# Two layers of attention over a key-value cache on one core: the last pair's sums moved ahead of the held chunks, a place of its own for five rows of wo, PV at the end of a turn, a K tile in four pieces

## The chip, the core and the metric

The kernel runs on one core of a Trainium2 chip. The core has a matrix engine (PE in the profile, with its weight loads as PEld), a vector engine (DVE), a scalar engine (ACT), a general engine (POOL), a queue that issues transfers (SP), and sixteen DMA engines that move data between the chip's memory and the core's own memory (SBUF). Matrix products land in a third, small memory (PSUM). The engines run side by side, each in the order of its own instructions, and wait for each other by semaphores. The metric is the device time of one execution in microseconds (us); less is better.

## What is computed

One token for each of two sequences goes through two layers. A layer adds an attention over a cache of 16384 keys in 32 heads, and then a block of two small matrices with a shift and an MLP with 4608 columns. Cut to what matters here:

```python
B, Sq, D = 2, 1, 576
H, Sk, Dh = 32, 16384, 128          # k_cache, v_cache: (B, H, Sk, Dh) in bf16

def _A_ref(x, k_cache, v_cache, wq, wo):
    q = (x @ wq).reshape(B, Sq, H, Dh).transpose(0, 2, 1, 3)
    scores = jnp.einsum("bhqd,bhkd->bhqk", q, k_cache) * (Dh ** -0.5)
    p = _softmax(scores, axis=-1)
    o = jnp.einsum("bhqk,bhkd->bhqd", p, v_cache)
    return o.transpose(0, 2, 1, 3).reshape(B, Sq, H * Dh) @ wo

def _B_ref(x, w1, w2, w3, w4):      # h = gelu(layernorm(x) @ w1), shifted by a token
    x1 = x + hs                     # hs = shifted h @ w2; with one token the shift leaves zeros
    return x1 + _gelu(_layernorm(x1) @ w3) @ w4

x = x + _A_ref(_layernorm(x), K, V, wq, wo)
x = x + _B_ref(_layernorm(x), w1, w2, w3, w4)
x = x + _A_ref(_layernorm(x), K, V, wq, wo)      # the same cache and weights again
x = x + _B_ref(_layernorm(x), w1, w2, w3, w4)
```

Both layers read the whole of K and V: 2 x 2 x 268 MB, which is nearly all of the 1093 MB that the profile counts.

## The kernel before, in words

**Tiles.** The 64 pairs of sequence and head are taken two heads at a time: 32 *pairs* in a layer. The K tile of a pair fills the 128 partitions, 64 for each head, with 256 keys of 128 numbers each in a partition: 65536 bytes in a partition, 8.39 MB in all. The V tile is as large. A tile is counted in 256 *blocks* (a block is one key in each partition, 256 bytes), and these in 8 groups of 32. SBUF holds three tile places (slots). K tiles take slots 0 and 1 in turn, V tiles have slot 2 alone, so the V tile of a pair can only be loaded when the V tile before it has been read.

**A pair's work** is written in `pair`. The blocks of the odd groups are scored on PE: `transposed` turns a chunk of 8 blocks (L1356), ACT copies it from PSUM to a small buffer (`evacuate`, L1362), and `scores` multiplies it with q (L1379), two chunks behind (`LEAD = 2`). There are 16 such chunks. The blocks of the even groups are scored on DVE: `dots` multiplies 16 blocks with q (L1391) and sums each over its 128 numbers (L1395), eight times in a pair; these are the *sums* of the title. Then come the maximum (`first_max` L1400, `softmax_max` L1408 and L1412, with a reduction over the partitions on POOL, L1414), the exponentials on ACT (L1423, L1429), and the q of the next pair (`q_column` L1305, `q_spread` L1312, `q_copy` L1317, which writes `qb`, read by the next pair's multiplications). The weights p then meet V one turn later: `pv` (L1448) is 256 small matmuls, and it stands in the turn of the pair after, behind the first three chunks:

```python
            if c == self.LEAD and s > 0:
                self.landed("v", self.order(l)[s - 1], False)
                for g in range(8):
                    self.pv(l, s - 1, g)
                self.tick()
```

So turn s holds the scores of pair s and the PV of pair s-1. `keep_o` (L1436) on DVE takes the result of PV away. Pairs 1 to 30 of layer 0, and 1 to 31 of layer 1, are turns of a real loop on PE, ACT and DVE (`Graph.loop`); `HEAD` gives the place of the loop's first PE instruction in a block of 256 instructions. SP and POOL have no loop; their instructions are written out. POOL passes on the landing of a tile (`landed`) to PE and DVE.

**Loads.** `plan_all` lists all loads in one order, and each carries the place that it fills. `Store.pump` adds the next load of the list to SP's queue as soon as, in the order of the program, the place is free (`used` and `release` free it in steps of two blocks). SP issues in that order and waits ahead of each load until the last readers of the place are done; a load that waits holds back all loads behind it. Where the last reader signals only its own engine or another one, SP waits for the next instruction of that engine that has a signal for all (`_stand_in`): for a multiplication of `dots` that is `first_max`. In a layer the order is K of pair s, V of pair s-1, K of pair s+1, and so on, and after the last V the weights wo, (w1,) w3, w4, and in layer 0 the wq of layer 1.

**The end of layer 0** is `closing` (pair 31, out of the loop) and `last_head` (PV of pair 31 and the product with wo). Pair 31's K and V stay in SBUF for layer 1, which starts with them, and so does the larger part of pair 30's K. To have more work early in layer 1, `ahead(l, HOLD)` turns the first four chunks of pair 31's K (blocks 0 to 31) a second time and leaves them in PSUM: the *held chunks*. That gives their cells free for a piece of wo. The place list of layer 0's wo has 76800 for the third piece (4608 bytes long); slot 1, where pair 31's K lies, starts at 73216, so the piece covers blocks 14 to 31. In `closing` the order is: sixteen chunks with half of PV 30 behind the eighth, then the held chunks, then the second half of PV 30, and then the eight `dots`. As the first two `dots` read blocks 0 to 31 and stand behind the load in the program, they wait for it, and read in blocks 14 to 31 what it wrote.

**The end of layer 1** is the last turn of the loop and `last_head`. wo comes in five pieces to slot 2: three of 8 rows, one of five rows and one of three (`WO_CUT = 5`; a row is 1152 bytes). The piece of five rows starts 3 rows ahead of the end of the 32 rows, so that it reaches two rows into the place of w1, which is next in the list:

```python
        self.plan_heads(1, [a, a + r8, a + 2 * r8, a + 4 * r8 - row * (self.HG - self.WO_CUT), a + 3 * r8])
        a += 4 * r8
        self.plan_small("w1", 1, self.w1, a, (0, 64))
```

w3's first two parts follow in slot 2, and the rest of w3 and all of w4 go to slot 0.

**The start of layer 1** is `opening` (pair 31 once more, from what was held), and then turn 1 with pair 30. The first tiles of the layer come in pieces (`FIRST`): what is missing of pair 30's K, then K of the third pair in eight pieces, V of pair 30 in three, and K of the fourth pair in two.

Of the kernel before, what the change touches and what calls it, by code (L numbers as in the profile page):

```python
# [356 lines left out]
class KB:  # L357
# [29 lines left out]
        [(0, 32768), (32768, 32768)],  # L387
# [166 lines left out]
    def plan_all(self):  # L554
# [38 lines left out]
        self.plan_heads(1, [a, a + r8, a + 2 * r8, a + 4 * r8 - row * (self.HG - self.WO_CUT), a + 3 * r8])  # L593
# [509 lines left out]
    def attention(self, l):  # L1103
        n = self.NP
        if l == 0:
            self.store.claim("kt", 0, self.AUX)
            self.q_column(0)
            self.q_spread(self.q_col, "q_col")
            self.q_copy()
            self.landed("k", self.order(l)[0], True)  # L1110
            self.pair(l, 0)
        else:
            self.opening(l)
        first = self.g.mark()
        end = n if l else n - 1
        for s in range(1, end):
            if l == 0 or s > 1:
                self.landed("k", self.order(l)[s], True)
            self.pair(l, s)
        self.g.loop(first, end - 1, 2, self.HEAD[l], self.TILE // 2 if l else -self.TILE // 2)  # L1120
# [14 lines left out]
    def pair(self, l, s):  # L1135
# [3 lines left out]
        def scores(c):  # L1139
            self.scores(self.kt[c % self.NKT], self.kt_keys(c % self.NKT), self.chunk_at(c), self.q_col, "q_col", ("s", c),  # L1140
                        last=c == 15)
        for c in range(16):
# [5 lines left out]
            if c == self.LEAD and s > 0:  # L1148
                self.landed("v", self.order(l)[s - 1], False)
                for g in range(8):  # L1150
                    self.pv(l, s - 1, g)
                self.tick()
        for c in range(16 - self.LEAD, 16):
            scores(c)
        for i in range(8):
# [10 lines left out]
    def closing(self, l):  # L1166
# [5 lines left out]
        self.landed("k", u, True)  # L1172

# [3 lines left out]
        for c in range(16):  # L1177
# [8 lines left out]
            if c == 7:  # L1186
                self.landed("v", v, False, (0,))
                for g in range(4):
                    self.pv(l, s - 1, g)
        for c in range(16 - self.LEAD, 16):  # L1190
            scores(c)
        self.ahead(l, self.HOLD)
        self.landed("v", v, False, (half,))
        for g in range(4, 8):
            self.pv(l, s - 1, g)
        self.tick()
        for i in range(8):
            self.dots(l, u, 2 * (i // 2) * self.GROUP + i % 2 * self.DB, i * self.DB)
        self.first_max(self.NB // 2)
# [334 lines left out]
```

## Time and profile before

| | |
|---|---|
| median of three runs | 2602.24 us (2601.66 to 2602.53) |
| the profiled execution | 2603.98 us, its span 2602.3 us |
| PE busy | 1623.4 us (62%) |
| DVE busy | 1901.5 us (73%) |
| ACT busy | 1173.3 us (45%) |
| DMA | 1093.05 MB, 420 GB/s over the span |
| mean granted PE clock | 0.642 |

The span runs from the first to the last instruction; the execution's own time is 1.7 us longer. Times within the trace count from the span's start. A busy share is a mean over stages that have different limits; in a stage the wait that ends last is what counts. A row of the timeline has the start, the duration, the engine, the line and the operation, and in brackets the idle time before it and what ended that. In a row of the windows the engines' busy times stand in the order PE, PEld, DVE, ACT, POOL, and the last three numbers are the granted PE clock, the share of the DMA engines and the GB/s that they moved.

### The profile page before, as it was taken

The page shows a single profiled execution, that of the slowest core. Times are in us where ns is not written, and L with a number is a line of the kernel's source. Part 1 is how long each engine was busy: PE and PEld are TensorE (multiplying, and loading weights), DVE is VectorE, ACT ScalarE, POOL GpSimd, SP SyncE. Part 2 cuts the span into 40 slices and gives each one's busy share as a digit, 9 for nine tenths or more (in the row PEclk, how much of TensorE's full clock was granted, in tenths as well). Part 3 has the DMA queues.
Part 4 walks back from the last instruction along what each step waited for, and adds up shares of the span by engine and source line. Part 5 has one row for each costly group of instructions (what it writes and reads, how often), then busy time and mean ns, then how long its engine had stood idle before and what let it go on. Part 6 is the DMA issues. An engine that isn't in the chain of part 4 may idle for free.

```text
span 2602.3 us, 82753 instructions
## 1 busy us (share of the span) xinstructions
PE 1623.4 (62%) x34418; PEld 1476.8 (57%) x34418; DVE 1901.5 (73%) x1598; ACT 1173.3 (45%) x1757; POOL 29.7 (1%) x101
## 2 busy tenths in 40 slices
PE   3657656656656656657268657657656656656656
PEld 2656556655655655656257546556556655655656
DVE  4887877877777777785428887877877877777772
ACT  2445445435435435435135445345445435435433
POOL 0000000000000000000000000000000000000000
PEclk9566666667666666656556667566666666656665
DMA  9999999999999999999489999999999999999997
GB/s 416 431 434 434 434 433 435 428 433 434 435 433 435 433 434 434 432 430 428 185 327 419 435 435 431 425 433 435 435 435 435 434 435 433 429 428 435 435 435 296
DMA packets 29364, 1093.05 MB, mean 420 GB/s; under 512 B 3210, under 2 KB 4876, under 8 KB 9612
## 3 DMA queue, kind: packets, MB, share of 16 engines
q1 hardware_dynamic: 29324, 1092.45, 97.5%
q8 instruction: 33, 0.54, 0.1%
q14 instruction: 7, 0.06, 0.0%
HBM read 1092.44 MB, written 0.00 MB: 420 GB/s over the span
## 4 chain that ended last, share of the span: by engine, by line
DMA 76%; PE 18%; issue 4%; ACT 1%; SPq 0%; DVE 0%; POOLq 0%; POOL 0%; DVEq 0%
DMA mem<-in_A_v_cache_dram 73%; PE mps L1448 17%; DMA mem<-in_B_w_dram 3%; SPq L99 0%; ACT mem L1362 0%; DMA mem<-in_A_wq_dram 0%; DMA mem<-in_A_k_cache_dram 0%; PE tps L1356 0%; DMA mem<-in_A_wo_dram 0%; PE sps L1001 0%; PE sps L928 0%; PE sps L1282 0%; PE mps L1001 0%; PE sps L1026 0%; ACT p L1429 0%
## 5 line engine op out<-in xcount | busy, mean ns | idle before, releaser
L1362 ACT ACTIVATE mem<-tps 128x1024 bf16<-128x1024 bf16 x996 | 981.8, 1027 | 1085.9 <-PE tps L1356 1071.6
L1395 DVE TENSOR_REDUCE s_dve<-prod 128x16 f32<-128x2048 bf16 x504 | 1152.2, 2286 | 17.3
L1356 PE MATMUL tps<-ident,mem 128*128 128x128 bf16 x8096 | 987.4, 259 | 55.8 <-issue 54.6
L1448 PE MATMUL mps<-p,mem 128*128 128x2 bf16 x16384 | 449.7, 165 | 639.3 <-POOLq L205 629.1
L1391 DVE TENSOR_TENSOR prod<-mem,qb 128x2048 bf16<-128x2048 bf16 x506 | 619.8, 1225 | 298.0 <-ACT qb L1317 189.2
L1356 PEld LDWEIGHTS tps<-ident,mem 128*128 (+1 forms) x8096 | 735.2, 110 | 177.7 <-issue 65.9
L1448 PEld LDWEIGHTS mps<-p,mem 128*128 128x128 bf16 x16384 | 444.3, 103 | 644.6 <-POOLq L205 634.0
L1379 PE MATMUL sps<-q_col,mem 128*128 128x2 bf16 x8064 | 367.2, 168 | 47.0 <-ACT mem L1362 44.6
L1379 PEld LDWEIGHTS sps<-q_col,mem 128*128 128x128 bf16 x8064 | 341.7, 102 | 55.5 <-ACT mem L1362 51.8
L1408 DVE TENSOR_REDUCE mx<-sps 64x1 f32<-64x128 f32 x128 | 37.1, 290 | 249.6 <-PE sps L1379 247.6
L1423 ACT ACTIVATE mx<-mx 64x1 f32<-64x1 f32 x128 | 25.7, 201 | 211.8 <-POOL mx L1414 210.3
L1312 PE MATMUL sps<-ident,q_col 128*128 128x128 bf16 x64 | 17.9, 279 | 119.3 <-DVE q_col L1305 119.3
L1312 PEld LDWEIGHTS sps<-ident,q_col 128*128 128x128 bf16 x64 | 6.6, 103 | 125.0 <-DVE q_col L1305 125.0
L1414 POOL PARTITION_ALL_REDUCE mx<-mx x64 | 25.0, 391 | 2512.7 <-DVE mx L1412 2512.7
L1429 ACT ACTIVATE p<-s_dve,mx 64x128 bf16<-64x128 f32 x126 | 50.3, 399 | 2.4
L1429 ACT ACTIVATE p<-sps,mx 64x128 bf16<-64x128 f32 (+1 forms) x130 | 46.1, 354 | 0.8
L928 PE MATMUL sps<-xn,mem 128*128 128x2 bf16 x544 | 21.3, 173 | 18.1 <-DMA mem<-in_B_w_dram 9.5
L1048 PE MATMUL sps<-share,prod 128*128 128x48 bf16 (+1 forms) x32 | 1.7, 195 | 48.1 <-DVE share L663 48.1
L928 PEld LDWEIGHTS sps<-xn,mem 128*128 128x128 bf16 x544 | 20.0, 119 | 19.2 <-DMA mem<-in_B_w_dram 10.1
L1048 PEld LDWEIGHTS sps<-share,prod 128*128 128x128 bf16 x32 | 1.3, 110 | 48.6 <-DVE share L663 48.6
L1317 ACT ACTIVATE qb<-sps 128x128 bf16<-128x128 f32 x65 | 18.0, 277 | 23.3 <-PE sps L1312 22.2
L670 ACT ACTIVATE sc<-sc 128x2 f32<-128x2 f32 x8 | 1.6, 203 | 57.5 <-DVE sc L667 57.5
(112 smaller groups left out, 304.4 us busy)
## 6 DMA issues: line engine op xcount, KB each, us to landing
mem<-in_A_v_cache_dram SPq DMA_DIRECT2D x5, 4096.0 KB, 18.8
mem<-in_A_k_cache_dram SPq DMA_DIRECT2D x10, 1024.0 KB, 7.9
mem<-in_A_wq_dram SPq DMA_DIRECT2D x8, 1024.0 KB, 16.4
mem<-in_A_k_cache_dram SPq DMA_DIRECT2D x2, 4096.0 KB, 16.7
mem<-in_B_w_dram SPq DMA_DIRECT2D x14, 576.0 KB, 7.3
mem<-in_B_w_dram SPq DMA_DIRECT2D x7, 864.0 KB, 17.9
mem<-in_B_w_dram SPq DMA_DIRECT2D x4, 1152.0 KB, 9.8
mem<-in_A_wo_dram SPq DMA_DIRECT2D x6, 576.0 KB, 15.4
```

Source lines behind the costliest of these rows:

```text
L928: ins = pe.matmul(out[:, m * B:(m + 1) * B], lhsT=buf[:, c:c + 127 * d + 1:d], rhs=self.xn[:, k, :], start=first and m == lo, stop=False, ...
L1312: self.pe(lambda pe: pe.matmul(self.sps[1][:, 256:384], lhsT=q[:, :], rhs=self.ident[:, :], start=True, stop=True, skip_group_check=True), ...
L1356: ins = pe.transpose(out[:, j * 128:(j + 1) * 128], self.g.slide(pe, self.mem, at + j * 128, 128), self.ident[:, :])
L1362: self.act(lambda e: e.activation(out=self.kt[k], in_=self.tps[t][:, :].rearrange("p (i c) -> p i c", i=self.CH), func=ACT.Copy), reads=[( ...
L1379: ins = pe.matmul(out[:, c0 + j, :], lhsT=kt[:, j, :], rhs=q[:, 0:128:64], start=True, stop=True, skip_group_check=True)
L1391: self.dv(lambda e: e.tensor_tensor(out=prod, in0=self.g.slide(e, self.mem, at, DB * 128).rearrange("p (j d) -> p j d", d=128), in1=qbc, o ...
L1395: self.dv(lambda e: e.tensor_reduce(out=sd[:, c0:c0 + DB], in_=prod, axis=AX.X, op=ALU.add), reads=["prod"], writes=[sk], to="vector")
L1408: self.dv(lambda e, p=p, a=a: e.tensor_reduce(out=self.mx[p, 1:2], in_=self.sps[0][p, a:a + n], axis=AX.X, op=ALU.max), reads=[("sps", 0)] ...
L1414: self.pool(lambda e: e.partition_all_reduce(self.mx[:, 4:6], self.mx[:, 2:4], channels=128, reduce_op=ROP.max), reads=[("mx2", 0), ("mx2" ...
L1423: self.act(lambda e, p=p, h=h: e.activation(out=self.mx[p, 6:7], in_=self.mx[p, 4 + h:5 + h], func=ACT.Copy, scale=-self.scale), reads=["m ...
L1429: self.act(lambda e, p=p, h=h, src=src, lo=lo, k=k, l=l: e.activation(out=self.p[p, h, lo:lo + k], in_=src, func=ACT.Exp, bias=self.mx[p, ...
L1448: ins = pe.matmul(self.mps[:, 448:450], lhsT=buf[:, j * 128:(j + 1) * 128], rhs=self.p[:, :, col], start=g == 0 and j == 0, stop=g == 7 an ...
```

## The change

There are four edits.

1. In `closing` the eight `dots` and `first_max` stand right behind the landing of pair 31's K, ahead of the chunks. The two halves of PV 30 stand behind the eighth and the twelfth chunk, each followed by a `tick` (one small matmul that carries a signal), so both precede the held chunks.
2. In layer 1 wo's piece of five rows starts where the third piece ends, and the piece of three rows behind it. Together they fill the 32 rows, and nothing reaches into w1's place.
3. In `pair`, PV of the pair before stands behind all chunks and their scores. Turn 1 of layer 1 alone keeps it behind the third chunk; it is taken out of the loop for that, so layer 1's loop has 30 turns, from pair 2 on, and its first slot changes (`flip`).
4. In `FIRST`, the fourth K tile of layer 1 comes in four pieces of 16384 bytes in a partition, where it came in two of 32768.

```diff
     FIRST = [
         REST,
         [(8192 * i, 8192) for i in (0, 1, 3, 5, 7, 2, 6, 4)],
         [(0, 8192), (8192, 24576), (32768, 32768)],
-        [(0, 32768), (32768, 32768)],
+        [(16384 * i, 16384) for i in range(4)],
     ]
...
-        self.plan_heads(1, [a, a + r8, a + 2 * r8, a + 4 * r8 - row * (self.HG - self.WO_CUT), a + 3 * r8])
+        self.plan_heads(1, [a, a + r8, a + 2 * r8, a + 3 * r8, a + 3 * r8 + row * self.WO_CUT])
...
         else:
             self.opening(l)
+            self.pair(l, 1, self.LEAD)
         first = self.g.mark()
-        end = n if l else n - 1
-        for s in range(1, end):
-            if l == 0 or s > 1:
-                self.landed("k", self.order(l)[s], True)
+        for s in range(l + 1, l + n - 1):
+            self.landed("k", self.order(l)[s], True)
             self.pair(l, s)
-        self.g.loop(first, end - 1, 2, self.HEAD[l], self.TILE // 2 if l else -self.TILE // 2)
+        self.g.loop(first, n - 2, 2, self.HEAD[l], -self.TILE // 2)
...
-    def pair(self, l, s):
+    def pair(self, l, s, at=None):
...
+        def ahead():
+            self.landed("v", self.order(l)[s - 1], False)
+            for g in range(8):
+                self.pv(l, s - 1, g)
+            self.tick()
         for c in range(16):
...
-            if c == self.LEAD and s > 0:
-                self.landed("v", self.order(l)[s - 1], False)
-                for g in range(8):
-                    self.pv(l, s - 1, g)
-                self.tick()
+            if c == at:
+                ahead()
         for c in range(16 - self.LEAD, 16):
             scores(c)
+        if s > 0 and at is None:
+            ahead()
...
     def closing(self, l):
...
         self.landed("k", u, True)
+        for i in range(8):
+            self.dots(l, u, 2 * (i // 2) * self.GROUP + i % 2 * self.DB, i * self.DB)
+        self.first_max(self.NB // 2)
...
-            if c == 7:
-                self.landed("v", v, False, (0,))
-                for g in range(4):
+            if c in (7, 11):
+                h = (c - 7) // 4
+                self.landed("v", v, False, (h * half,))
+                for g in range(4 * h, 4 * h + 4):
                     self.pv(l, s - 1, g)
+                self.tick()
         for c in range(16 - self.LEAD, 16):
             scores(c)
         self.ahead(l, self.HOLD)
-        self.landed("v", v, False, (half,))
-        for g in range(4, 8):
-            self.pv(l, s - 1, g)
-        self.tick()
-        for i in range(8):
-            self.dots(l, u, 2 * (i // 2) * self.GROUP + i % 2 * self.DB, i * self.DB)
-        self.first_max(self.NB // 2)
         self.keep_o(s - 1)
```

## The prediction

> **What bounds the kernel now.** I read the page's slices first, then windows around each slice that is below the rest, then the timelines of the engines in these windows and the waits of SP's queue.
>
> ```profile
> GB/s 416 431 434 434 434 433 435 428 433 434 435 433 435 433 434 434 432 430 428 185 327 419 435 435 431 425 433 435 435 435 435 434 435 433 429 428 435 435 435 296
> ...
> 1044.50:1083.20 38.70, 24.34 (x519) 22.51 (x517) 29.64 (x24) 18.00 (x27) 0.38 (x1) 0.63 1.00 434
> 1245.00:1255.00 10.00, 8.86 (x181) 8.59 (x181) 0.00 (x0) 0.00 (x0) 0.00 (x0) 0.67 0.41 151
> 1273.00:1311.00 38.00, 8.17 (x270) 8.04 (x271) 27.84 (x26) 5.80 (x15) 1.23 (x1) 0.50 0.00 1
> 2556.70:2570.00 13.30, 10.44 (x331) 10.07 (x328) 2.53 (x16) 0.00 (x0) 0.00 (x0) 0.50 0.09 25
> 2570.00:2597.00 27.00, 13.74 (x340) 12.99 (x340) 4.31 (x31) 5.56 (x11) 2.32 (x13) 0.50 1.01 405
> ```
>
> In the loops the DMA engines are full: a turn of 38.7 us moves its two tiles at 434 GB/s with a share of 1.00, while no engine is busy for more than 30 of the 38.7. So a turn can't get shorter, and time lies only where the DMA stands still: 38 us between the layers (1 GB/s), some 6 us just ahead of that (151 GB/s), and 12.5 us near the end (13.3 us at 25 GB/s hold 0.8 us of transfer). A tile takes half a turn, 19.35 us.
>
> Why the 38 us: DVE.
>
> ```profile
> 1198.91 7.01 PE L1448 MATMUL mps<-p,mem 128*128 128x2 bf16 x256 [11.38 <-POOLq L205]
> 1221.29 0.23 DVE L1305 COPY q_col<-q_f 128x128 bf16 x1
> 1235.10 0.83 PE L1448 MATMUL mps<-p,mem 128*128 128x2 bf16 x26 [1.36 <-issue]
> 1252.11 0.33 SPq L99 DMA_DIRECT2D mem<-in_A_v_cache_dram  x1
> 1268.44 1.22 DVE L1391 TENSOR_TENSOR prod<-mem,qb 128x2048 bf16<-128x2048 bf16 x1 [46.92 <-DMA mem<-in_A_wo_dram]
> 1294.75 2.29 DVE L1395 TENSOR_REDUCE s_dve<-prod 128x16 f32<-128x2048 bf16 x1
> 1298.08 0.32 DVE L1412 TENSOR_TENSOR mx<-mx 64x1 f32<-64x1 f32 x2
> 1304.36 6.83 PE mps L1448 x256
> 1311.19 1.16 PE sps L1001 x40
> ```
>
> DVE ends its loop at 1221.5 and then waits 46.9 us, for a landing of wo. By the code that is the piece over blocks 14 to 31, which the program loads ahead of the sums. The sums run from 1268.4 to 1297.0 (28.6 us), and maximum, exponentials, PV 31 (1304.4) and the product with wo (1311.2) follow in a chain. All further loads hang on that product, so the DMA is idle.
>
> **Edit 1, the sums first (T1).** They now need only pair 31's K and `qb`. V29 had landed when PV 29 began (1198.91, freed by POOL), so K31 lands 19.35 us later, at 1218.3, V30's halves at 1227.9 and 1237.6. `qb` isn't later than K31, since the turn ends earlier (edit 3, below). The sums end at 1218.3 + 28.6 = 1247. PE: chunks come each 1.07 us (below), so half a PV (3.5) can start at 1227.9 and the other at 1237.6, each with the 1.36 of idle "issue" that this row shows, which is instruction supply; the remaining chunks, scores and held chunks end at 1248 to 1252. V31's second half, issued at 1252.1 before, is issued at about 1242.5, inside the transfer of the first, which closes the hole at 1245 to 1255; it lands at 1237.6 + 19.35 = 1256.9. Maximum at 1249.4 in place of 1298.4, PV 31 six us later, at 1255.4, its second half at 1258.9; end 1262.4, with a stall of 1.4 1263.8. Against 1311.2 that is **T1 = -47.4**. What is late next is V31's landing: had the sums ended at 1253, the end would be the same within a microsecond or two. The cost that moves: wo's piece over blocks 14 to 31 must now wait for `first_max` (1247) and PE's instruction behind the held chunks (1253), with three pieces behind it in SP's queue. That is covered by V31, in flight until 1256.9, and the two pieces ahead; six pieces (3.5 MB, 8 us) land by 1265, as the product reaches them. Without that cover it would cost up to 8. Bounds: -48.8 without a stall; -40 with two stalls of 2.1 and 3.5 (rows below) and 3 of waiting for wo.
>
> **Edit 2, wo's five rows (T4).**
>
> ```profile
> SPq L99 <- PE sps L1001: 35.3, 1, 35.3
> ...
> 2529.39 3.36 SPq L99 DMA_DIRECT2D mem<-in_A_wo_dram  x5
> 2567.69 13.63 SPq L99 DMA_DIRECT2D mem<-in_B_w_dram  x15
> ...
> 2527.46 7.02 PE L1448 MATMUL mps<-p,mem 128*128 128x2 bf16 x256 [11.25 <-POOLq L205]
> 2553.87 4.02 PE L1448 MATMUL mps<-p,mem 128*128 128x2 bf16 x144
> 2559.26 3.13 PE L1448 MATMUL mps<-p,mem 128*128 128x2 bf16 x112 [1.38 <-issue]
> 2571.34 0.17 DVE L660 TENSOR_TENSOR xn<-prod,sc 128x10 bf16<-128x10 f32 x1 [0.27 <-ACT sc L670]
> 2575.77 1.73 PE L928 MATMUL sps<-xn,mem 128*128 128x2 bf16 x36 [4.02 <-DMA mem<-in_B_w_dram]
> 2578.62 1.72 PE L928 MATMUL sps<-xn,mem 128*128 128x2 bf16 x36 [1.13 <-DMA mem<-in_B_w_dram]
> ```
>
> SP waited 35.3 us for a product with wo (L1001), with fifteen weight loads behind it; the DMA idled 12.5 us. Without the overlap w1 and w3's first parts go out behind wo at PV's end (2534), the rest at the last `first_max` (by 2544), all ahead of wo's end at 2556.7. So **T4 = -12.5**. The transfer (27 us at 405 GB/s) still bounds: PV 31 starts at V31's landing (2527.5 + 19.35 = 2546.8) and ends at 2555, `xn` follows in 9 us as now (2562.4 to 2571.3), at 2564, when w3's second piece lands; a piece costs PE 1.7 us and the DMA 2.85 (the two rows of L928 start so far apart), so PE catches up. Bounds: -13.3, and -9 if it doesn't quite.
>
> **Edit 3, PV last.** The rows that carry it are those of the first turns, of layer 0 and then of layer 1.
>
> ```profile
> 72.17 3.39 PE L1356 MATMUL tps<-ident,mem 128*128 128x128 bf16 x24 [0.62 <-issue]
> 81.39 3.57 PE L1448 MATMUL mps<-p,mem 128*128 128x2 bf16 x128 [2.13 <-issue]
> 88.42 0.61 PE L1448 MATMUL mps<-p,mem 128*128 128x2 bf16 x17 [3.46 <-issue]
> 88.92 1.01 PE L1356 MATMUL tps<-ident,mem 128*128 128x128 bf16 x8
> 89.98 1.01 PE L1356 MATMUL tps<-ident,mem 128*128 128x128 bf16 x8
> 89.09 0.33 SPq L99 DMA_DIRECT2D mem<-in_A_v_cache_dram  x1
> 105.37 0.38 PE L1379 MATMUL sps<-q_col,mem 128*128 128x2 bf16 x8 [0.71 <-ACT mem L1362]
> 105.78 0.61 DVE L1408 TENSOR_REDUCE mx<-sps 64x1 f32<-64x128 f32 x2 [1.48 <-PE sps L1379]
> 110.17 1.22 DVE L1391 TENSOR_TENSOR prod<-mem,qb 128x2048 bf16<-128x2048 bf16 x1 [3.17 <-ACT qb L1317]
> 115.16 7.01 PE L1448 MATMUL mps<-p,mem 128*128 128x2 bf16 x256 [3.28 <-POOLq L205]
> ...
> 1402.10 1.16 SPq L99 DMA_DIRECT2D mem<-in_A_k_cache_dram  x2
> 1405.04 3.33 PE L1356 MATMUL tps<-ident,mem 128*128 128x128 bf16 x24 [0.86 <-POOLq L205]
> 1415.48 0.33 SPq L99 DMA_DIRECT2D mem<-in_A_v_cache_dram  x1
> 1416.35 12.97 ACT L1362 ACTIVATE mem<-tps 128x1024 bf16<-128x1024 bf16 x13 [6.92 <-PE tps L1356]
> 1443.30 7.01 PE L1448 MATMUL mps<-p,mem 128*128 128x2 bf16 x256 [0.71 <-POOLq L205]
> ```
>
> In the steady turn PV last costs nothing. K lands at T; DVE's eight sums take 29.6 (DVE's time in the window of 38.7), and from the maximum to the next pair's first multiplication go 4.4 (105.78 to 110.17), so the next turn is ready at T + 34 of 38.7: a margin of 4.5. PE: sixteen chunks at 1.07 (88.92 to 89.98) and the last scores to T + 18.6, V lands at T + 19.35, PV ends at T + 26.4, when the next V load is issued, as now; the DMA wants it at T + 38.7, a margin of 12. I take **T7 = 0**. In the first turns it costs something, because there the turn runs late and PV holds the V load.
>
> Layer 0, turn 1 (T2): V1 is issued at 89.1, waits behind K2, and has landed at 115.1, so its transfer started at 95.7. With PV last, the other thirteen chunks start at 76.0 (three chunks, 3.4, and a score from 72.2 on) where they started at 88.9; they took 16.9 us (to 105.75), so PV begins at 92.9. It takes 7.0 in the loop, and in this first pass 2.1 and 3.5 more, idle at "issue". The queue is empty this time from 95.7 on, for which the nearest row is the 1.38 near the end (DMA idle); I take 8.4. PV ends at 101.3, V1 is issued 0.2 later, and data flow 1.5 after an issue (at the end: issue at 2567.7, and 0.8 us of transfer by 2570). The DMA stands from 95.7 to 103.0: **T2 = +7.3**, between 3.5 (thirteen chunks in 14.5, as ACT's 12.97 for thirteen copies with the scores behind gives, and no stall) and 11.5 (both stalls). It is paid once: turn 2 starts by DVE, as now, and its PV ends at 133 (first chunk 107, as now, + 18.6 + 7.0), ahead of K3's end at 141.
>
> Layer 1, turn 2 (T3): the V load issued at 1415.5 has landed by 1443.3, so it started at 1423.9. With PV last the thirteen chunks start at 1408.6, end at 1423.1 to 1425.5, PV ends 7.0 to 8.4 later, in the loop's first pass; with issue and start 1.7: 1434.3. **T3 = +10.4**, between 7.9 and 15.8.
>
> By the Trainium skill (Runtime: NRT & Kernel Launch, "Instruction fetch mechanics") crossing a 16 KiB boundary of code is mostly hidden; the first pass above does not bear it out. By that rule T1 would be -48.8, T2 5.9, T3 9, and the sum would give 2556.
>
> **Edit 4, four pieces (T6).** Both pieces are issued together at 1402.1, behind `first_max`, for which SP waits whatever the piece; four will be too, at 0.58 us each, with the first under way. **T6 = 0**, between -1.5 (the gap at that place closes) and +1.2.
>
> **Sum.** -47.4 - 12.5 + 7.3 + 10.4 = -42.2, on a span of 2602.3. The profiled execution took 2603.98, the median is 2602.24, so the durations stand for the median within 0.1%. Forecast: 2560.0 us. The bounds add up to -52 and -20.5: 2550 to 2582. From run to run the times differ by under 0.05%, so 0.2% (5 us) is what I call a change.
>
> **Rivals.**
> - *The starts cost nothing*: V1 and its counterpart hide behind something I don't see; 2602.2 - 59.9 = 2542. Against it: SP's queue holds no load that could pass them. 0.08.
> - *The gains are partly given back*: instruction supply stalls PE in `closing`, `last_head` and both first passes, and the bounds all fall badly; 2582. The stalls of 2.1 and 3.5 speak for it. 0.16.
> - *Slower: the sums still start late.* If another landing or signal ahead of the sums takes the place of wo's, T1 is zero and 2602.2 + 17.7 - 12.5 = 2607. It decides as soon as T1 is under 5 us. Against it: by the code the first multiplication needs K31 and `qb` alone. 0.06.
> - *Slower: the turn no longer fits.* DVE's chain of 34 us would have to grow by over 4.5; each microsecond beyond costs 60 turns, so 0.7 beyond eats the whole gain, and one gives 2620. Against it: no instruction is added to the chain, and PV's end (T + 26.4) is ahead of `keep_o`'s turn (T + 30). 0.05.
>
> **Chances.** The forecast has 0.65, its own range being 2552 to 2569; with the second rival it fills 2550 to 2582. I give 2546 to 2582. Faster by over 0.2%: 0.65 + 0.08 + 0.16 = 0.88, rounded; slower 0.10; the same 0.02.
>
> **What would show it.** In the changed trace DVE's wait for wo should be gone, and the sums of pair 31 should start within 2 us of its K's landing; the window without transfer between the layers should shrink from 38 us to under 4; the 25 GB/s window near the end should vanish, with the weight loads issued ahead of V31's landing; and two new windows without transfer, 5 to 11 us long, should stand near 96 us and in layer 1's third pair, each ended by PV's end. Turns of 38.7 us throughout would bear out T7. Wrong it would be if turns are longer, or if DVE still waits in `closing`.

## The result, and the profile after

| | before | after |
|---|---|---|
| median | 2601.95 us (2599.72 to 2602.53) | 2560.77 us (2560.33 to 2562.96) |
| ratio | | 0.9845, interval 0.9828 to 0.9862 |
| span of the profiled execution | 2602.3 us | 2558.6 us |
| DVE busy | 1901.5 us | 1896.2 us |
| DMA | 1093.05 MB, 420 GB/s | 1093.13 MB, 427 GB/s |
| mean granted PE clock | 0.642 | 0.678 |

The forecast was 2560.0 us. The changed kernel moves the same data and does the same work; the span of its profiled execution is 43.7 us shorter, because the DMA stands still for less time. The medians differ by 41.2 us: the profiled execution of the kernel before took 2603.98 us, 2 us over its median. These are the slices of the page and some windows around its weak places (columns as in the prediction):

```profile
GB/s 413 379 429 440 426 443 426 441 428 435 433 430 439 426 442 427 441 428 433 401 408 378 426 442 427 434 434 427 442 426 442 427 441 428 434 434 428 441 426 383
...
90.00:95.00 5.00, 3.23 (x116) 3.05 (x113) 4.79 (x4) 1.02 (x1) 0.00 (x0) 0.64 0.65 279
95.00:100.00 5.00, 3.94 (x142) 3.87 (x143) 4.82 (x3) 0.00 (x0) 0.00 (x0) 0.50 0.02 3
100.00:105.00 5.00, 0.80 (x31) 0.71 (x27) 4.68 (x8) 0.00 (x0) 0.00 (x0) 0.50 0.82 292
1386.00:1389.00 3.00, 3.00 (x116) 3.00 (x114) 2.82 (x3) 0.00 (x0) 0.00 (x0) 0.50 0.02 5
1440.00:2490.00 1050.00, 672.72 (x13974) 591.37 (x13972) 805.12 (x626) 511.80 (x736) 10.22 (x27) 0.68 1.00 433
```

The slices of 185 and 327 GB/s in the middle are 401 and 408 now, and the last one went from 296 to 383. Two slices that were nearly full (431 and 419), the second (379) and the twenty-second (378), have a hole each, at 95 to 100 us and around 1387 us. In between the steady turns keep the DMA full (a share of 1.00, 433 GB/s over 1050 us).

The timeline of the changed kernel where the 38 us without transfer stood (DVE, PE, then SP's queue):

```profile
1226.36 1.23 DVE L1393 TENSOR_TENSOR prod<-mem,qb 128x2048 bf16<-128x2048 bf16 x1 [7.36 <-POOLq L205]
1252.68 2.29 DVE L1397 TENSOR_REDUCE s_dve<-prod 128x16 f32<-128x2048 bf16 x1
1256.66 0.32 DVE L1414 TENSOR_TENSOR mx<-mx 64x1 f32<-64x1 f32 x2
...
1246.10 3.58 PE L1450 MATMUL mps<-p,mem 128*128 128x2 bf16 x128 [2.30 <-POOLq L205]
1262.53 4.27 PE L1450 MATMUL mps<-p,mem 128*128 128x2 bf16 x152
1268.61 2.91 PE L1450 MATMUL mps<-p,mem 128*128 128x2 bf16 x104 [1.81 <-issue]
1274.52 0.59 PE L1001 MATMUL sps<-share,mem 128*128 128x2 bf16 x16 [2.36 <-issue]
...
1239.54 10.54 SPq L99 DMA_DIRECT2D mem<-in_A_v_cache_dram  x2
1250.11 25.35 SPq L99 DMA_DIRECT2D mem<-in_A_wo_dram  x8
1362.22 2.22 SPq L99 DMA_DIRECT2D mem<-in_A_k_cache_dram  x4
```

DVE no longer waits 46.9 us for wo. It waits 7.4 us for POOL's word that pair 31's K has landed, and sums from 1226.4 to 1255.0. The maximum stands at 1256.7, PV 31 starts at 1262.5 and ends at 1271.5. The fourth K tile of layer 1 is issued at 1362.2 instead of 1402.1.

### The profile page after: what moved, and what is told of

It is laid out like the page before. It is cut to its first block, busy times and chain, and to the rows that moved or that the text cites. A ratio compares the mean times of both kernels' runs of the same rounds, so it can differ in the third digit from the quotient of the medians.

```text
span 2558.6 us, 82601 instructions
## 1 busy us (share of the span) xinstructions
PE 1630.7 (64%) x34419; PEld 1441.1 (56%) x34419; DVE 1896.2 (74%) x1598; ACT 1206.9 (47%) x1757; POOL 30.8 (1%) x101
## 2 busy tenths in 40 slices
DMA packets 29658, 1093.13 MB, mean 427 GB/s; under 512 B 3242, under 2 KB 4908, under 8 KB 9644
## 4 chain that ended last, share of the span: by engine, by line
DMA 64%; DVE 18%; PE 11%; issue 5%; ACT 1%; DVEq 0%; POOL 0%; POOLq 0%; SPq 0%; ACTq 0%
DMA mem<-in_A_v_cache_dram 38%; DMA mem<-in_A_k_cache_dram 25%; DVE s_dve L1397 12%; PE mps L1450 9%; DVE prod L1393 6%; PE tps L1358 1%; DMA mem<-in_B_w_dram 1%; PE sps L928 0%; PE sps L1001 0%; DMA mem<-in_A_wq_dram 0%; PE mps L1001 0%; DVEq L131 0%; ACT p L1431 0%; DVE mx L1402 0%; DVEq L126 0%
## 5 line engine op out<-in xcount | busy, mean ns | idle before, releaser
L1358 PE MATMUL tps<-ident,mem 128*128 128x128 bf16 x8096 | 999.4, 246 | 400.1 <-POOLq L205 395.4
L1364 ACT ACTIVATE mem<-tps 128x1024 bf16<-128x1024 bf16 x996 | 1009.4, 1025 | 345.7 <-PE tps L1358 331.0
L1381 PE MATMUL sps<-q_col,mem 128*128 128x2 bf16 x8064 | 358.1, 167 | 48.1 <-ACT mem L1364 45.9
L1381 PEld LDWEIGHTS sps<-q_col,mem 128*128 128x128 bf16 x8064 | 322.8, 99 | 57.4 <-ACT mem L1364 56.4
L1410 DVE TENSOR_REDUCE mx<-sps 64x1 f32<-64x128 f32 x128 | 36.5, 285 | 6.7 <-PE sps L1381 4.7
L928 PE MATMUL sps<-xn,mem 128*128 128x2 bf16 x544 | 20.9, 173 | 11.4 <-DMA mem<-in_A_wq_dram 8.6
L1438 DVE COPY o_acc<-mps 128x2 f32 (+1 forms) x64 | 10.2, 160 | 22.8 <-PE mps L1450 20.8
L1431 ACT ACTIVATION_READ_ACCUMULATOR p<-sps,mx (+1 forms) x130 | 24.4, 188 | 0.0
```

What stands on the lines that cost most here:

```text
L928: ins = pe.matmul(out[:, m * B:(m + 1) * B], lhsT=buf[:, c:c + 127 * d + 1:d], rhs=self.xn[:, k, :], start=first and m == lo, stop=False, ...
L1358: ins = pe.transpose(out[:, j * 128:(j + 1) * 128], self.g.slide(pe, self.mem, at + j * 128, 128), self.ident[:, :])
L1364: self.act(lambda e: e.activation(out=self.kt[k], in_=self.tps[t][:, :].rearrange("p (i c) -> p i c", i=self.CH), func=ACT.Copy), reads=[( ...
L1381: ins = pe.matmul(out[:, c0 + j, :], lhsT=kt[:, j, :], rhs=q[:, 0:128:64], start=True, stop=True, skip_group_check=True)
L1410: self.dv(lambda e, p=p, a=a: e.tensor_reduce(out=self.mx[p, 1:2], in_=self.sps[0][p, a:a + n], axis=AX.X, op=ALU.max), reads=[("sps", 0)] ...
L1431: self.act(lambda e, p=p, h=h, src=src, lo=lo, k=k, l=l: e.activation(out=self.p[p, h, lo:lo + k], in_=src, func=ACT.Exp, bias=self.mx[p, ...
```

## The experiments

The first four make one edit, or a part of one, on the kernel before; the others alter the changed kernel. Runs 2, 3 and 4 keep the order in which pair 31's first two sums read wo's bytes; in all the others they read K, as in the changed kernel.

**1. Only the sums first.**

```diff
         self.landed("k", u, True)
+        for i in range(8):
+            self.dots(l, u, 2 * (i // 2) * self.GROUP + i % 2 * self.DB, i * self.DB)
+        self.first_max(self.NB // 2)
...
-        for i in range(8):
-            self.dots(l, u, 2 * (i // 2) * self.GROUP + i % 2 * self.DB, i * self.DB)
-        self.first_max(self.NB // 2)
```

> The kernel before with one thing changed: in closing, the eight dots and first_max stand right behind the landing of pair 31's K. PV keeps its places. Theory 1 (the wait for wo's piece is what held the sums, and nothing takes its place): DVE's 46.9 us of waiting go, the sums run from about 1224 to 1253; V31's second half is still issued at 1252, because the second half of PV 30 stands behind the held chunks, so it lands near 1264 and PV 31 ends near 1269 instead of 1311: 2602 - 42 = 2560 us (2556 to 2564), and a hole of some 6 us in the transfers ahead of it stays. Theory 2 (the gain comes from PV standing last, which lets a pair's work end ahead of the next landing; without it another wait takes the place of this one): 2590 or more.

Measured: 2563.59 us, ratio 0.9856 (0.9839 to 0.9872). Just inside the range. The first sum and the next tile's issue, in the timeline of this kernel:

```profile
1224.29 1.23 DVE L1391 TENSOR_TENSOR prod<-mem,qb 128x2048 bf16<-128x2048 bf16 x1 [2.82 <-ACT qb L1317]
...
1361.30 1.27 SPq L99 DMA_DIRECT2D mem<-in_A_k_cache_dram  x2
```

The issue moved from 1402.1 to 1361.3, by 40.8 us (by 38.6 against run 4, below). Here the sums don't wait for the tile but for `qb`, since PV, early in the turn before, pushed that turn's end back. The median is 37.2 us below the kernel before beside it, where the whole change gains 41.2: nearly the whole gain lies in this half of edit 1.

**2. Only wo's place.** One line: the place list of the five pieces, as in the diff above.

> The kernel before with only the place of wo's five rows in layer 1 changed. Theory 1 (the overlap with w1's place is the only reason for the 12.5 us without transfer near the end): the weight loads go out ahead of V31's landing, the hole goes, and as PV 31 starts as late as before (2553.9) the vector xn is ready at 2571 or, with instruction supply slower beside a full queue, at 2575; from there to the end the changed kernel takes 18.4: 2590 to 2594 us. Theory 2 (the hole is only moved, because PE and not the transfer sets the end once the loads are early): 2597 or more.

Measured: 2594.99 us, ratio 0.9979 (0.9970 to 0.9989), 5.8 us against the 2600.79 of the kernel before beside it. That is a gain, 1 us short of the range and under half of the 12.5 us that the prediction gave to this edit. The hole itself is gone: the DMA moves 403 and 421 GB/s in the two stretches of 10 us from 2550 on. But PV 31 starts no earlier than before (2551.79 us), and from `xn` on PE waits for no piece of the weights, so PE sets the end, as theory 2 has it. Where the rest lies is shown by run 5.

**3. Only PV last**, with layer 1's first turn out of the loop.

> The kernel before with only PV moved to the end of the turn (turn 1 of layer 1 out of the loop with its early PV, as in the changed kernel); closing, wo's place and the pieces are as before. Theory 1 (PV last costs the two holes in the first turns, 7.8 and 8.8 us, and gives back the lag at the ends of the layers: closing starts 4 to 5 us earlier in the transfers' time, and PV 31 of layer 1 some 7 us): +16.6 - 4.9 - 6.7 = +5, that is 2607 us (2602 to 2612), with the holes near 95 us and in layer 1's third pair. Theory 2 (PV last is what gains): under 2590.

Measured: 2610.84 us, ratio 1.0040 (1.0025 to 1.0054): the edit alone makes the kernel slower, by some 10 us, at the upper end of the range. Against the trace of run 4, which is the kernel before in all but its four pieces, it loses 7.7 us in layer 0's first turn and 8.1 in layer 1's third pair, and wins back 4.6 between the layers and only 2.8 in the tail.

**4. Only the four pieces.**

> The kernel before with only the fourth K tile of layer 1 in four pieces. Theory 1 (all pieces wait for the same first_max): all four are issued within 2.3 us at 1402, the hole of 1.5 us there stays, 2602 us within 2. Theory 2 (smaller pieces start earlier): the hole goes and 1.5 to 3 us with it.

Measured: 2601.26 us, ratio 1.0001 (0.9991 to 1.0010). No effect, as forecast. The issue of the four pieces, and PV 31 of layer 1, in the timeline of this kernel:

```profile
1399.86 1.84 SPq L99 DMA_DIRECT2D mem<-in_A_k_cache_dram  x4
...
2553.87 6.98 PE L1448 MATMUL mps<-p,mem 128*128 128x2 bf16 x256
```

Up to this issue runs 2 and 4 do what the kernel before does, and both issue at 1399.9 us. So the 1402.1 of the kernel before holds some 2.2 us that belong to its one profiled execution and not to the kernel.

**5. All but PV last**: the changed kernel with PV early in every turn.

```diff
-            self.pair(l, s)
+            self.pair(l, s, self.LEAD)
         self.g.loop(first, n - 2, 2, self.HEAD[l], -self.TILE // 2)
```

> The changed kernel with PV behind the third chunk in every turn, as before the change; the loops, the sums first, wo's place and the four pieces stay as changed. Theory 1: the holes of 7.8 and 8.8 us in the first turns go, and the lag at the layers' ends comes back (closing starts 4 us later in the transfers' time, which V31's landing partly covers; PV 31 of layer 1 7 us later, which the full queue partly covers): 2561 - 16.6 + 1 to 8 = 2545 to 2553 us, faster than the changed kernel. Theory 2 (the gain needs PV last): 2561 or more.

Measured: 2555.19 us, ratio 0.9823 (0.9807 to 0.9839): 5.6 us faster than the changed kernel (5.2 by the two spans), though 2 us short of the range. The two intervals overlap, but all four times lie below all four of the changed kernel (2554.0 to 2555.8 against 2560.3 to 2563.0). Without edit 3 the change is better. The timeline of this kernel (SP's queue, then PE at the end):

```profile
1202.51 41.48 SPq L99 DMA_DIRECT2D mem<-in_A_v_cache_dram  x4
1358.18 3.25 SPq L99 DMA_DIRECT2D mem<-in_A_k_cache_dram  x4
2486.89 3.36 SPq L99 DMA_DIRECT2D mem<-in_A_wo_dram  x5
...
2485.00 6.98 PE L1450 MATMUL mps<-p,mem 128*128 128x2 bf16 x256 [11.43 <-POOLq L205]
2511.14 3.99 PE L1450 MATMUL mps<-p,mem 128*128 128x2 bf16 x144
```

Against it, and by the same issues, the changed kernel is late by 8.0 us at the end of layer 0 (1210.46), by 4.0 at 1362.22, by 11.4 at 2498.27 and by 5.2 at the end of the span. So edit 3 costs 8.0 and 7.3 us in the two holes, and gives 3.9 back between the layers and 6.2 in the tail (2.8 in run 3, where edit 2 is missing). The tail: with PV early, PE stands 11.4 us before V of pair 30 has landed, with thirteen chunks of the last pair behind that wait, and PV 31 starts only at 2511.1.

**6. PV early in the first turns only**: two more turns of each layer written out with PV early, the loops (28 turns) with PV last.

```diff
+        for s in range(l + 1, l + 3):
+            self.landed("k", self.order(l)[s], True)
+            self.pair(l, s, self.LEAD)
         first = self.g.mark()
-        for s in range(l + 1, l + n - 1):
+        for s in range(l + 3, l + n - 1):
```

> The changed kernel with PV early (behind the third chunk) in turns 1 and 2 of layer 0 and 1 to 3 of layer 1, written out ahead of the loops; from there on PV last, in loops of 28 turns. Theory 1 (the holes come from the V load that waits for a late PV, and a turn wins 4 us on the transfers until it has caught up): both holes go, nothing comes back, 2561 - 16.6 = 2544 us (2541 to 2548). Theory 2 (the holes belong to the first pass through a loop's code, not to PV's place): they stay, one pass later, 2556 or more.

Measured: 2556.03 us, ratio 0.9825 (0.9809 to 0.9841). A miss: the rival's range. The holes at 95 and 1387 us are gone, but others stand in the first turns of the loops. Windows and timeline of layer 1:

```profile
1455.00:1459.00 4.00, 1.75 (x66) 1.66 (x63) 3.82 (x3) 0.00 (x0) 0.00 (x0) 0.50 0.40 168
1459.00:1463.00 4.00, 2.72 (x96) 2.64 (x96) 1.44 (x2) 0.00 (x0) 0.00 (x0) 0.50 0.02 4
...
1430.81 3.24 PE L1361 MATMUL tps<-ident,mem 128*128 128x128 bf16 x24 [3.21 <-issue]
1453.18 3.57 PE L1453 MATMUL mps<-p,mem 128*128 128x2 bf16 x128 [0.43 <-issue]
1460.19 2.70 PE L1453 MATMUL mps<-p,mem 128*128 128x2 bf16 x95 [3.44 <-issue]
1523.73 6.99 PE L1453 MATMUL mps<-p,mem 128*128 128x2 bf16 x256 [0.89 <-POOLq L205]
```

In the loop's first pass PE is idle at "issue" inside PV; two passes later (the last row) the same 256 matmuls run without a break. Two causes were open: these stalls, or the lag with which the turn begins.

**7. The second half of PV 30 behind the held chunks again**, as in the kernel before, with all else changed.

> The changed kernel with the second half of PV 30 in closing back behind the held chunks; the sums stay first. Theory 1 (V31's second half is then issued about 12 us later and its landing sets PV 31's end): a hole of 5 to 7 us in the transfers near 1258, 2561 + 6 = 2567 us (2563 to 2571). Theory 2 (the sums and the softmax set PV 31's start, V31's landing has room): 2561.

Measured: 2562.78 us, ratio 0.9854 (0.9838 to 0.9871): 2 us behind the changed kernel, which is less than a measurement tells apart, and by the time nearer to the rival. The trace shows theory 1's mechanism at a smaller size (SP's queue, PE, and a window):

```profile
1255.21 0.33 SPq L99 DMA_DIRECT2D mem<-in_A_v_cache_dram  x1
...
1268.89 3.58 PE L1452 MATMUL mps<-p,mem 128*128 128x2 bf16 x128 [3.02 <-POOLq L205]
...
1250.00:1260.00 10.00, 7.29 (x176) 6.83 (x173) 8.95 (x15) 2.06 (x10) 1.23 (x1) 0.73 0.84 328
```

V31's second half is issued 5.5 us later than in the changed kernel (1249.74), not 12. The transfers lose some 2.4 us (328 GB/s instead of 434 for 10 us), and the second half of PV 31 waits 3.0 us for this landing, where the changed kernel has a stall of 1.81. So V31's landing has hardly any room.

**8. Two more sums**: in every turn the first of the eight sums is done three times, for 7.4 us more on DVE. The result is the same.

> The changed kernel with the first of a pair's eight sums done three times instead of once, in every turn (7.4 us more on DVE; the result is the same). Theory 1 (DVE's chain of 34 us has a margin of 4.5 in a turn of 38.7): a turn grows by about 2.9 us, 58 turns by 168, so about 2730 us. Theory 2 (the margin is larger, the chain overlaps the next landing): under 2600. Theory 3 (there is hardly any margin): 2900 or more.

Measured: 2763.7 us, one run. More than the forecast of 2730, but with a margin clearly there. The steady turn tells it best, as SP's queue shows:

```profile
1703.86 0.33 SPq L99 DMA_DIRECT2D mem<-in_A_v_cache_dram  x1
1745.37 0.33 SPq L99 DMA_DIRECT2D mem<-in_A_v_cache_dram  x1
```

A turn takes 41.5 us. A sum is 1.22 + 2.29 us and the gaps, 3.69 in all (two added ones start at 1722.31 and 1726.00 us); less two of them the chain is 34.1, and the margin to 38.7 is 4.6 us. The profile counts the added sums in 62 pairs (x124), not in the 58 turns of the expectation: at 2.8 us each they add 174 of the 203 us. In a layer's first pairs the addition shows whole (the first K that is held back is issued at 77.41 us, 7.3 later than in the changed kernel); the rest was not followed further.

**9. One more sum** in every turn, 3.7 us.

> The changed kernel with the first of a turn's eight sums done twice (3.7 us more of VectorE in each of 58 turns; the result is the same). Done three times it cost 203 us, 3.5 us of 7.4 a turn. Theory: a steady turn has some 3.9 us of room on VectorE, so that one more sum is nearly hidden: 2561 to 2566 us. Rival: about half of any added work shows: some 2660 us.

Measured: 2566.04 us, ratio 0.9863 (0.9847 to 0.9880): 5.3 us over the changed kernel, at the upper edge of the range, and some 95 us under the rival. The added sums are 218 us of DVE's busy time in 62 pairs, and nearly all of it is hidden. While layer 0 catches up, its turns come 38.0 us apart (V's issues at 177.50 and 215.49 us), which gives 34.3 to the chain without the addition. What shows comes where a turn is late: the first V that is held back is issued at 104.61 us (100.84 in the changed kernel), and layer 1's fourth K tile 7.4 us later than there, with hardly more lost up to the last V (7.7).

**10. Six turns early** in place of two in run 6; the loops have 24 turns.

> The changed kernel with PV early in six more turns at the head of each layer, written out, and late in the loops' remaining 24 turns. With only two such turns the holes in the transfers at 95 and 1384 us went, but others came in the first turn of each loop (V issued at 173.81 and at 1462.96 us, 4 GB/s in 1459-1463). Theory: that turn began 7 to 10 us behind the landing of its K, since the lag of the layer's start was made up by only some 4 us in each turn (38.7 us of transfers against about 34.7 us of VectorE's work), and the turn is also long, as TensorE waits some 9 us for instructions the first time that it goes through the loop. With six turns the lag is made up before the loop, V is issued about 33 us behind the landing of K where the queue lasts 38.7, and no hole is left: 2554.0 less about 8 us in layer 1 and 2 to 4 in layer 0, a time of 2546 us (2542 to 2550). Rival: a turn with the loop's instructions new to TensorE cannot be fed in time whatever it starts with; then the holes stay, moved by four turns, and the time is 2555 us or more.

Measured: 2560.04 us, ratio 0.9848 (0.9831 to 0.9864). A second miss, and the rival's number: the holes moved to the loops' first turns again. The timeline of layer 0 there, and the windows:

```profile
272.87 6.96 PE L1453 MATMUL mps<-p,mem 128*128 128x2 bf16 x255 [9.07 <-POOLq L205]
283.90 0.16 PE L1453 MATMUL mps<-p,mem 128*128 128x2 bf16 x1 [4.07 <-issue]
299.88 3.42 PE L1361 MATMUL tps<-ident,mem 128*128 128x128 bf16 x24 [0.52 <-issue]
331.50 0.33 SPq L99 DMA_DIRECT2D mem<-in_A_v_cache_dram  x1
...
324.00:328.00 4.00, 2.56 (x97) 2.48 (x93) 3.70 (x3) 0.00 (x0) 0.00 (x0) 0.50 0.70 299
328.00:332.00 4.00, 1.17 (x38) 1.09 (x38) 3.88 (x5) 0.00 (x0) 0.00 (x0) 0.50 0.29 119
```

But the trial had not set up its own condition. With PV early PE waits for V in each turn (9.07 us) and has thirteen chunks to do behind it, so the next turn always begins late, and no lag is made up; my 4 us a turn were wrong. V landed at 272.9, so the loop's first K landed a tile later, at 292.2, and its first chunk began 7.7 us behind that, 4.1 of it from a stall at the end of the last written-out PV. V was issued 31.6 us after that chunk, 39.3 us behind the K, when the queue of two tiles (38.7 us) was empty.

**11. PV last in layer 1's last turn alone**: loops with PV early, layer 1's last two turns written out.

```diff
+        end = l + n - 1 - 2 * l
         first = self.g.mark()
-        for s in range(l + 1, l + n - 1):
+        for s in range(l + 1, end):
             self.landed("k", self.order(l)[s], True)
-            self.pair(l, s)
+            self.pair(l, s, self.LEAD)
...
+        for s in range(end, l + n - 1):
+            self.landed("k", self.order(l)[s], True)
+            self.pair(l, s, self.LEAD if s < n - 1 else None)
```

> The changed kernel with PV early in every turn but the last of layer 1; that layer's last two turns are written out. With PV early in all turns (2555.19 us) TensorE stood 11.4 us before V30 had landed at 2485.0 us, with 13 of the turn's 16 chunks behind that wait, and the end was set by TensorE: PV31 started at 2511.14 us though its V had room to land by 2504. Theory: with PV last in this one turn the chunks fill that wait, the softmax of pair 31 is ready some 6 us sooner, and the time is 2549 us (2545 to 2552). Rival: the written-out turns keep TensorE waiting for instructions, by 7 us a turn, and give the gain away: 2554 to 2560 us.

Measured: 2552.08 us, ratio 0.9814 (0.9797 to 0.9830), between theory and rival: 3.1 us faster than with PV early throughout (3.5 by the two spans; the intervals overlap), where 6.2 were to be had. The written-out turns have the stalls; PV 30, for one, is cut in two:

```profile
2488.86 4.25 PE L1454 MATMUL mps<-p,mem 128*128 128x2 bf16 x154
2495.71 2.86 PE L1454 MATMUL mps<-p,mem 128*128 128x2 bf16 x102 [2.60 <-issue]
```

**12. Two loops in a layer**: 14 turns with PV early, then 16 with PV last.

```diff
+        half = l + n // 2 - 1
         first = self.g.mark()
-        for s in range(l + 1, l + n - 1):
+        for s in range(l + 1, half):
             self.landed("k", self.order(l)[s], True)
-            self.pair(l, s)
-        self.g.loop(first, n - 2, 2, self.HEAD[l], -self.TILE // 2)
+            self.pair(l, s, self.LEAD)
+        self.g.loop(first, half - l - 1, 2, self.HEAD[l], -self.TILE // 2)
+        first = self.g.mark()
+        for s in range(half, l + n - 1):
+            self.landed("k", self.order(l)[s], True)
+            self.pair(l, s)
+        self.g.loop(first, l + n - 1 - half, 2, self.HEAD[l], -self.TILE // 2)
```

> The changed kernel with two loops in each layer: PV early in the first (14 turns), late in the second (16 turns). The written-out early turns of the last trial made up nothing: they took some 39.4 us each (K issued at 256.64 and 295.99 us) against 38.7 of transfers, so the first late turn again began 11 us behind the landing of its K (transfers ran dry at about 327.5, so that K landed at 288.8, and the first chunk began at 299.88). Looped early turns do make it up: with PV early throughout, chunks began some 4.5 us behind the landing of K in the layer's last turn. Theory (hole from the lag and the first pass together): the second loop's first turn issues its V 4.5 + 31.6 = 36.1 us behind the landing of K, where the queue lasts 38.7 less some 2.6 of restart, so no hole of more than 2 us opens; the tail is that of the changed kernel, and the time is 2547 us (2543 to 2552). Rival (the first pass with PV last opens its hole whatever the lag): holes of 5 to 8 us near 600 and 1900 us in each layer and a time of 2556 us or more.

Measured: 2549.43 us (2548.73 to 2550.49), ratio 0.9799 (0.9782 to 0.9815), inside the range, the fastest of all and 11.3 us below the changed kernel. Timeline of layer 0, and windows of both switches:

```profile
579.70 6.99 PE L1456 MATMUL mps<-p,mem 128*128 128x2 bf16 x256 [11.17 <-POOLq L205]
603.75 3.37 PE L1364 MATMUL tps<-ident,mem 128*128 128x128 bf16 x24 [1.19 <-issue]
627.06 3.57 PE L1456 MATMUL mps<-p,mem 128*128 128x2 bf16 x128 [2.13 <-issue]
634.36 1.15 PE L1456 MATMUL mps<-p,mem 128*128 128x2 bf16 x37 [3.72 <-issue]
635.57 0.33 SPq L99 DMA_DIRECT2D mem<-in_A_v_cache_dram  x1
...
632.00:636.00 4.00, 1.17 (x38) 1.09 (x38) 3.40 (x5) 0.00 (x0) 0.00 (x0) 0.50 0.84 360
1918.00:1922.00 4.00, 2.72 (x96) 2.64 (x96) 3.26 (x7) 0.00 (x0) 0.00 (x0) 0.50 0.65 250
```

The stalls of the first pass are all there (2.13 and 3.72 us within PV, as in run 10's 1.68 and 3.72), and the turn is as long: 31.8 us from the first chunk to V's issue. But V landed at 579.7, the K so at 599.05, and the first chunk began 4.7 us behind that instead of 7.7. V is issued 36.5 us behind the K, and of the holes only 0.7 us (360 GB/s instead of 434 for 4 us) and 1.7 us are left. (By the end of the transfers instead of the landing that PE sees, each lag is some 3 us larger, which is the 11 us of the expectation.) So the first pass alone opens hardly any hole here; with a start 3.0 us later run 10 lost some 4 us in layer 0. The stalls alone were not taken away in any run; how much would go with them is open.

## Why the prediction was right, point by point

- **T1, the sums first: -47.4 forecast, -47.7 between the two profiled executions, some -45.5 for the kernels.** The fourth K tile's issue moved by 39.9 us, with T2's 7.8 against it. But by runs 2 and 4 the kernel before issues that tile at 1399.9 and not at 1402.1, so 2.2 us of the 47.7 belong to that one execution, and that the size agrees to 0.3 us is luck. The steps held, some 7 to 8 us later than written because of T2: K31 at 1226.2 (1218.3 forecast), PV 31's start at 1262.5 (1255.4) and its end at 1271.5 (1263.8). The wait for wo that moved behind `first_max` cost nothing visible; one stall of 1.8 us in PV 31 stood where 1.4 was assumed, and one of 2.4 in the product with wo behind it was not foreseen. The 1.4 us given to each half of PV 30 did not come. The prediction's maximum stands 1 us later behind the sums (1249.4 after 1247) than the rows of the kernel before give (1.4 us, 1297.0 to 1298.4), and no row carries that microsecond; in the changed kernel it ends 2.0 us behind them. Run 1 shows how the sum is shared: 38.6 us, counted from run 4's issue, come from the sums' place alone. Of the other 6.9, run 5 gives 3.9 to edit 3, by which `qb` is ready ahead of K31, and leaves 3.0 to the place of PV 30's halves; run 7, which puts the second half back, finds 1.9 at the same issue (1364.13).
- **T4, wo's place: -12.5 forecast, -12.6 measured, but put down to the wrong edit, and the size is luck.** The offset to the kernel before went from -31.1 us at the last V to -43.7 at the end. Run 2 gives edit 2 alone 5.8 us, and run 5 shows that 6.2 us of the tail come with edit 3. Run 11, with PV last in the last turn alone, gained 3.1 of them. The prediction's step "PV 31 starts at V31's landing" holds only with PV last; with PV early the chunks queue behind V of pair 30, and that is edit 3's doing. The tail also came out otherwise than written, at the same price by chance. These are its rows in the changed kernel:

```profile
2515.83 3.98 PE L1450 MATMUL mps<-p,mem 128*128 128x2 bf16 x144 [3.56 <-POOLq L205]
2521.67 3.15 PE L1450 MATMUL mps<-p,mem 128*128 128x2 bf16 x112 [1.86 <-issue]
2527.57 0.81 PE L1001 MATMUL sps<-share,mem 128*128 128x2 bf16 x25 [2.36 <-issue]
2534.03 0.94 PE L1001 MATMUL sps<-share,mem 128*128 128x2 bf16 x29 [2.16 <-issue]
2538.53 6.38 PE L928 MATMUL sps<-xn,mem 128*128 128x2 bf16 x144
...
2501.68 35.86 SPq L99 DMA_DIRECT2D mem<-in_B_w_dram  x15
```

  The weight loads are issued from 2501.7 on, but only two of the fifteen ahead of V31's landing (PV 31 starts at 2515.8); the second takes 14.1 us to issue, and the others follow up to 2537.5. The DMA engines stay full all the same (a share of 1.02, 412 GB/s from 2515 to 2537). But `xn` is ready 13.7 us behind the end of PV 31 (2524.8 to 2538.5), not 9, for more stalls at "issue". By then w3 has landed, and 144 matmuls run without a wait, where the kernel before waited for a piece after every 36. PE, not the transfer, sets the end, where the prediction had written that the transfer still bounds.
- **T2, layer 0's first turn: +7.3 forecast, +7.8 measured** (V's issues stay 7.80 to 7.94 us late from the third on). V1 is issued at 100.84 where 101.5 was worked out.

```profile
100.84 0.33 SPq L99 DMA_DIRECT2D mem<-in_A_v_cache_dram  x1
1390.36 0.33 SPq L99 DMA_DIRECT2D mem<-in_A_v_cache_dram  x1
```

- **T3, layer 1's second pair: +10.4 forecast, +8.8 measured**, inside its bounds of 7.9 to 15.8. V's issue at 1390.36 is 2.5 us earlier than forecast once the shift is taken off (1434.3 less 1.5 for the start and 39.9 gives 1392.9), as the chunks were done at the early end of their range (1383.0) and PV had a stall of 0.28 us only. The Trainium skill (Runtime: NRT & Kernel Launch, "Instruction fetch mechanics"), by which code crossings are mostly hidden, would have had T2 at 5.9 and T3 at 9: the trace goes against it in layer 0 (7.8, with 1.96 us of "issue" in PV) and not in layer 1 (8.8, with 0.28).
- **T6, four pieces: 0 forecast; 1.0001 in run 4.** The four are issued together behind `first_max`, over 2.22 us.
- **T7, the steady turn: 0 forecast, 0.1 us of drift in 26 turns.** The forecast gave 34 us to the chain of a turn; runs 8 and 9 give 34.1 and 34.3, and run 9 hides one more sum.
- **The rivals.** The steady turn rules out the turn that doesn't fit, and the start of the sums at 1226.4, with K31, rules out another signal ahead of them. The two holes rule out that the starts cost nothing. The stalls of the second rival did come, of 1.8 to 2.4 us each, but not all terms went to their bad bounds.

What the prediction did not see is that edit 3 is a loss on balance in this kernel. It priced the two holes nearly right (17.7 us forecast, 16.6 measured), but counted the edit's gains in T1 and T4. By run 5 it costs 15.3 us and gives back 10.1. The total, 2560.0 us against 2560.77, came closer than the terms: T3 was 1.6 us too high, T1 some 2 us too large a gain.

## What to carry to other kernels

When several edits are made together, price each by what the tail and the stage boundaries look like without it; a gain that two edits share will otherwise be put down to one of them. Compare the trace of the kernel before with a second trace of the same work, as run 4's here: one execution was 2 us off. In this kernel, moving a consumer to the end of a turn costs nothing where the turn waits for its data, and costs the transfer queue a hole in each turn that starts late; so use the late order only once the turns start on time, for which a second loop (run 12) is cheap. An experiment should show in its own trace that it set up its condition; run 10 did not, and its time alone would have settled the question the wrong way.

## What the runs showed of the hardware

PE stands still at "issue" for up to 4.1 us at a time in code that it meets for the first time, inside runs of matmuls that wait for nothing, and not in later turns of the same loop (run 6: 3.44 us in the first pass, none in the third). Where two stalls follow each other in PV, 128 matmuls lie between them (run 12: 2.13 and 3.72 us, run 6: 0.43 and 3.44); with their weight loads these are 256 instructions of PE.

The stalls come with full transfers. PV 31 of layer 1 and the product with wo behind it are the same instructions in all runs but for their places. In the changed kernel, with the DMA at 412 GB/s from 2515 to 2537, they hold stalls of 1.86, 2.36 and 2.16 us; in run 2 (413 GB/s) of 2.07, 2.64 and 1.89, in run 5 (404 GB/s) of 1.85, 2.63 and 1.89. In the kernel before, whose hole lies there (105 GB/s from 2553 to 2568), they are 1.38 and 0.17, and in run 4 (66 GB/s) there are none: its 256 matmuls of PV 31 take 6.98 us without a break. Run 1, which keeps that hole, has none either, and runs 6 to 12, which have lost it, have all three. So once the hole was closed, the code that had run in it took some 5 to 6 us longer. I had not expected it in such amounts.

I take the stalls for the supply of instructions, in pieces of 256, which is slower beside full transfers. The first passes, the even distance and the full transfers speak for it, but it is not shown: no run changed that supply itself, and `HEAD`, which places a loop's code, was left alone. The written-out turns of runs 10 and 11 have such stalls (4.07 and 2.60 us), and the 2.60 us of run 11 lie in the last PV ahead of its tail; what else kept it from the 6.2 us that it was after is open.
